# A gated mix of linear attention and a bilinear GLU: other h blocks in the joint products, no negated copies of o in DRAM, PSUM banks taken by age, the last two joint products behind the last unit

## The chip, the cores and the metric

The kernel runs on one core of one Trainium2 chip. The core has a matrix engine (TensorE, PE in the profile, with its weight loads as PEld), a vector engine (VectorE, DVE), a scalar engine (ScalarE, ACT), GpSimd (POOL) and a queue engine (SyncE, SP) that only issues DMA transfers. POOL issues the transfers that add to their destination. Each engine works through its own instructions in the order in which they stand, and waits for others through semaphores. The metric is the device time of one execution in microseconds, taken as the median of several runs.

## The reference

With x of 2048 x 512, everything in float32:

```
g = sigmoid((x * gate_w).sum(-1))                 # one number per row
q, k, v = x @ wqkv, split into 32 heads of 16     # phi(t) = where(t > 0, t + 1, exp(t)) + 1e-6
kv = phi(k)^T v per head;  z = sum of phi(k)
o = phi(q) kv / (phi(q) z + 1e-6)
a = o @ wo                                        # 512 x 512
h = (x @ w_gate) * (x @ w_up)                     # 512 -> 1792 columns
b = h @ w_down                                    # 1792 -> 512
out = g * a + (1 - g) * b
```

So a linear attention and a bilinear feed-forward layer read the same x, and their outputs are mixed by a gate.

## The kernel before

**Three products for one.** Every float32 operand is split into a high part (float32r) and the remainder, and a product is made of three matmuls: high x high, high x low, low x high (`mm3`, line 94). Splits cost one copy on ACT and one subtraction on VectorE.

**Seven products for eight.** Products of blocks of 2 x 2 are made by Strassen's scheme in Winograd's form: sums of blocks are formed first, seven products are taken, and their results are combined. This is done in two places.

**Units.** After a first phase (k, v and the attention's state), the work is a list `order` of 32 units, 16 for each half of the rows of x (pair 0 is units 0 to 15, pair 1 units 16 to 31). A unit (`unit`, line 415) makes one block of 128 columns: an `f` unit one block of h (both the gate and the up projection), a `q` unit two blocks of q. In pair 1 the units are f0, q0, f1, f2, f3, q1, f4 to f13, that is, the q units are 17 and 21, and f4 to f7 are units 22 to 25. The seven products go to four banks Y, X, R and S, in the order Y, X, Y, R, X, R, S, each of six matmuls of 512 columns. Between them ACT copies `m` (from the first Y) and `cross` (from the second Y and the second X), and VectorE forms `t`, the R and the S sums. Thus a delay of ACT at `m` stops the second Y, and a delay of `cross` stops the next use of the bank X or Y.

**Places.** Side work is hung on named places in a unit: `low`, `e`, `m`, `c`, `d`, `t`, `s`, `r`, `end`, in this order. `later(n, place, fn)` registers it, `do(n, place)` performs it. `d` is where the weights of the unit after next are prepared: `w_add` (line 165) has ACT scale and copy in the tile `wr`, which SP loaded at the end of the unit before (`w_load`, line 158), and then POOL adds other blocks into it by DMA.

**Down jobs.** Two f blocks of h and their rows of w_down make a group, and a group is 8 down jobs (`down_jobs`, line 649), one for each 128 rows of the output: six matmuls of 512 columns (two blocks, three each) into one bank `pdn`, which VectorE then adds to the sum `acc` in SBUF, scaled by 1 - g. Each unit performs as many as `shares` (line 407) gives for its four spots: after the first X (`many[0]`), after the second Y, after the second X, and before the second R.

**Attention.** A q unit leaves phi(q). In the next units the denominators are formed through DRAM (`terms`, `den`), and four tiles `rb` come back; VectorE multiplies them with phi(q) to give o (`norm_end`, line 744), and SP stores o in DRAM (`opark`). For the blocks 11 and 22 of o ACT also makes a negated copy in the tile `phq`, stored as `-11` and `-22`. For the last q unit of pair 1 these steps fall in units 24 and 25.

**Joint products.** The product of o with its weight (wo folded into the attention's state, blocks `wraw` in DRAM) is again a 2 x 2 scheme of seven products (`OPROD`, line 51; `products`, line 772). In pair 1 the scheme is shared with four h blocks, `MIXED` (line 37), f4 to f7, which go through the same combination: h is scaled by (1 - g)/g (`keep_scale`), so that one accumulation holds both. Those four units get no down jobs; their h stays in the tiles `hraw`. In pair 1 a joint product is four jobs of twelve matmuls of 256 columns, two with h (kind `h`) and two with o (kind `o`), into two banks `po`; then VectorE adds the banks to `acc`. Two of the seven continue in the banks of the one before. Each job k has its steps: the weight is loaded by SP (`w_raw`), added to by POOL (`w_sum`) and split (`w_split`); the o block is loaded by SP (`load`, k - 5), added to by POOL (`add`, k - 3) and split (`ready`, k), where k counts steps of five to a unit in pair 1 and four in pair 0. `step0` (line 775) says where step 0 lies: in pair 1 the place `e` of unit 26.

**Rings.** Tiles of one tag share a ring of buffers: `z`, `ph` (four each) and `cb` (three) hold `rb`, phi(q), the loaded o blocks `oraw` and the weights `wraw` in turn. A load into a ring waits until the buffer's last user is done, stores to DRAM included, and whatever stands behind it in SP's queue waits too.

**Banks.** Beside Y, X, R and S there are four PSUM banks, two with the tag `dn` and two with `att`. Down jobs and joint products take them by alternating the tag (`banks.reverse()`, line 668 and line 853), within the tag in turn.

**The end.** Behind the last unit stand the low parts of its h and the 8 down jobs of the last group (lines 994 to 998).

Of the kernel before, what the change touches and what calls it, by code (L numbers as in the profile page):

```python
# [14 lines left out]
P = 128  # L15
S = 2048
D = 512
# [19 lines left out]
MIXED = ((), (4, 5, 6, 7))  # L37
# [26 lines left out]
def gated_mix(ctx: ExitStack, tc, xt, xp, x, wqkv, wq, wq_add, wo, wgu, wgu_add, wdn, gate_w, out):  # L64
# [326 lines left out]
    ojobs, passed = [], [0]  # L391

# [251 lines left out]
    banks = ["dn", "dn"]  # L644
# [4 lines left out]
    def down_jobs(pair, group):  # L649
# [3 lines left out]
        def job(i):  # L653
# [12 lines left out]
            for o in range(0, D, step):  # L666
                cols = slice(o, o + step)
                banks.reverse()
                pd = psum.tile([P, D], F32, tag=banks[0], name="pdn", bufs=2)[:, 0:step]
                for j, (((_, hh), (_, hl)), (_, w2)) in enumerate(group):  # L670
                    mm3(pd, (hh[:, c, sl], hl[:, c, sl]), [w2[:, v, cols] for v in range(2)], j == 0, j == 1)
                a = acc[pair, i // 2][:, i % 2, cols]
                if first:
                    act(a, pd, scale=s)
                else:
                    stt(a, pd, s, a, ALU.mult, ALU.add)
                if ends:
                    to = nc.gpsimd if pair == 0 else nc.sync
                    tc.keep_in_program_order(to.dma_start(out[t * P:(t + 1) * P, cols], a))
            todo[0] -= 1  # L680
            if not todo[0]:
# [7 lines left out]
             for b in ("11", "12", "21", "22", "-11", "-22")}  # L689

    def attention(pair, j, n):
# [80 lines left out]
    def products(pair, n0):  # L772
        raw, tiles, wt, bank = {}, {}, {}, {}
        steps = STEPS[bool(MIXED[pair])]
        step0 = len(steps) * n0 + (0 if MIXED[pair] else 2)
# [13 lines left out]
        def load(k):  # L789
            p, kind, i = line[k]  # L790
            if kind == "o":
                dma(raw_tile(k).rearrange("p (r t) -> p r t", r=2), opark[pair, OPROD[p][2][0]][i])
# [36 lines left out]
        def ready(k, place):  # L829
            p, kind, i = line[k]  # L830
            tiles[k] = hi, lo = o_tiles()
            if k in raw:
                split(hi, lo, raw.pop(k))
            else:
                (block,) = OPROD[p][2]
                sign = -1.0 if block[0] == "-" else 1.0
                act(hi, row(block, i), scale=sign)
                if sign > 0:
                    tt(lo, row(block, i), hi.bitcast(F32), ALU.subtract)
                else:  # L840
                    stt(lo, row(block, i), -1.0, hi.bitcast(F32), ALU.mult, ALU.subtract)
            ojobs.append((passed[0] - (place == "end"), lambda: job(k)))

        def job(k):
# [5 lines left out]
            def product(h, s, lhs, r, starts, stop):  # L850

                if starts and not goes_on and s == 0:
                    banks.reverse()
                    bank[h] = psum.tile([P, 2, HALF], F32, tag=banks[0], name="po", bufs=2)
                mm3(bank[h][:, s], lhs, [v[:, r] for v in w2], starts and not goes_on and s == 0, stop, True)
# [11 lines left out]
            for block, sign in sums:  # L867
                m, c = int(block[0]) - 1, int(block[1]) - 1
                a = acc[pair, 2 * c + i][:, :, m * HALF:(m + 1) * HALF]
                tt(a, a, bank[i], ALU.add if sign > 0 else ALU.subtract)  # L870
# [91 lines left out]
    half = None  # L962
    for n, (pair, kind, m) in enumerate(order):
        entry = {}
        if n == 4:

            banks[0] = "att"
# [27 lines left out]
    down(0)  # L995
# [54 lines left out]
```

## Time and profile before

| | |
|---|---|
| median of 3 runs | 616.66 us (616.22 to 617.41) |
| profiled execution | 615.53 us, of which its span 613.8 us |
| TensorE busy | 598.3 us, 97% |
| VectorE busy | 461.9 us, 75% |
| ScalarE busy | 332.7 us, 54% |
| mean granted TensorE clock | 0.997 |
| moved by DMA | 116.04 MB, mean 189 GB/s |

The span runs from the first to the last instruction. A row of a timeline gives the start and the length in us, the engine, the line (L72 is the matmul's helper, L78 that of activations, L81 and L84 those of VectorE, L102 and L105 the two for transfers), the tiles as output<-inputs, and in brackets the idle time of that engine before the instruction, with what ended it. Tiles have the program's names without numbers. A row of the windows gives the stretch, its length, the busy time of PE, PEld, DVE, ACT and POOL with the instructions of each, the granted clock, the busy share of the DMA engines and GB/s. A row of waits gives the total, the count and the longest. Unit n starts with its first Y product, `bY<-xah`: unit 24 at 440.23, unit 25 at 451.11, unit 26 at 462.07, unit 27 at 487.03, unit 31 at 575.31.

### The profile page before, as it was taken

The page shows a single profiled execution, that of the slowest core. Times are in us where ns is not written, and L with a number is a line of the kernel's source. Part 1 is how long each engine was busy: PE and PEld are TensorE (multiplying, and loading weights), DVE is VectorE, ACT ScalarE, POOL GpSimd, SP SyncE. Part 2 cuts the span into 40 slices and gives each one's busy share as a digit, 9 for nine tenths or more (in the row PEclk, how much of TensorE's full clock was granted, in tenths as well). Part 3 has the DMA queues.
Part 4 walks back from the last instruction along what each step waited for, and adds up shares of the span by engine and source line. Part 5 has one row for each costly group of instructions (what it writes and reads, how often), then busy time and mean ns, then how long its engine had stood idle before and what let it go on. Part 6 is the DMA issues. An engine that isn't in the chain of part 4 may idle for free. (4 is left out here: it accounts for less than half of the span.)

```text
span 613.8 us, 8334 instructions
## 1 busy us (share of the span) xinstructions
PE 598.3 (97%) x2898; PEld 499.2 (81%) x2898; DVE 461.9 (75%) x736; ACT 332.7 (54%) x580; POOL 76.2 (12%) x95
## 2 busy tenths in 40 slices
PE   9999999999999999999999999999996989999997
PEld 6888888888888888888888888887874878888885
DVE  6877896756787788787789976677884777778955
ACT  3856756579546745453635567568353555345320
POOL 0011100000111110222201220001003311211000
PEclk9999999999999999999999999999998999999999
DMA  9467949657779878999688857687769988844003
GB/s 298 163 196 134 289 94 274 155 166 199 210 173 272 209 198 230 281 255 211 180 218 235 178 154 197 180 237 183 175 161 286 235 194 215 207 77 104 2 0 137
DMA packets 65803, 116.04 MB, mean 189 GB/s; under 512 B 7969, under 2 KB 29985, under 8 KB 65697
## 3 DMA queue, kind: packets, MB, share of 16 engines
q1 hardware_dynamic: 52816, 77.50, 38.1%
q0 software_dynamic: 12656, 37.49, 34.1%
q10 hardware_dynamic: 288, 0.52, 0.3%
q8 instruction: 22, 0.36, 0.2%
q14 instruction: 21, 0.16, 0.1%
HBM read 97.65 MB, written 19.94 MB: 192 GB/s over the span
## 5 line engine op out<-in xcount | busy, mean ns | idle before, releaser
L72 PE MATMUL pdn<-slot,slot 128*128 128x512 f32 (+1 forms) x582 | 144.9, 388 | 0.9 <-DVE slot L81 0.9
L72 PEld LDWEIGHTS pdn<-slot,slot 128*128 128x128 f32 x582 | 107.4, 188 | 23.2 <-DVE slot L81 1.6
L84 DVE SCALAR_TENSOR_TENSOR acc<-pdn,gate,acc 128x512 f32<-128x512 f32 (+1 forms) x81 | 59.7, 741 | 22.3 <-PE pdn L72 21.7
L81 DVE TENSOR_TENSOR wcl<-wr,wch 128x512 fp32r<-128x512 f32 (+1 forms) x96 | 73.4, 773 | 1.6 <-ACT wch L78 1.4
L78 ACT ACTIVATE slot<-cross 128x512 fp32r<-128x512 f32 x48 | 30.2, 629 | 81.1 <-DVE cross L81 81.1
L78 ACT ACTIVATE wch<-wr 128x512 fp32r<-128x512 f32 (+1 forms) x96 | 60.5, 695 | 0.7 <-DMA wr<-in_wgu_add 0.6
L72 PE MATMUL bX<-xbh,wch 128*128 128x512 f32 x128 | 50.3, 393 | 4.0 <-ACT cross L78 4.0
L105 POOL DMA_DIRECT2D wr<-in_wgu_add x28 | 24.1, 859 | 222.4 <-ACT wr L78 174.1
L72 PE MATMUL bX<-xbh,wcl 128*128 128x512 f32 x128 | 50.3, 393 | 0.0
L72 PE MATMUL bX<-xbl,wch 128*128 128x512 f32 x128 | 50.3, 393 | 0.0
L72 PE MATMUL po<-owh,oh 128*128 128x256 f32 x168 | 47.4, 282 | 1.7 <-DVE acc L81 1.7
L72 PE MATMUL po<-owh,ol 128*128 128x256 f32 x168 | 47.8, 285 | 0.8 <-DVE ol L81 0.8
L72 PE MATMUL po<-owl,oh 128*128 128x256 f32 x168 | 47.5, 283 | 0.0
L78 ACT ACTIVATE cross<-bY 128x512 f32<-128x512 f32 x32 | 19.1, 597 | 48.2 <-PE bY L72 48.0
L78 ACT ACTIVATE wr<-wr 128x512 f32<-128x512 f32 x64 | 36.6, 623 | 12.7 <-DMA wr<-in_wgu 9.4
L81 DVE TENSOR_TENSOR t<-bR,cross 128x512 f32<-128x512 f32 x32 | 22.1, 690 | 27.2 <-PE bR L72 18.2
L78 ACT ACTIVATE cross<-bX 128x512 f32<-128x512 f32 x32 | 19.0, 595 | 33.3 <-DVE bS L81 33.3
L81 DVE TENSOR_TENSOR bR<-bX,m 128x512 f32<-128x512 f32 x32 | 22.3, 697 | 19.0 <-PE bX L72 16.2
L72 PEld LDWEIGHTS po<-owh,oh 128*128 128x128 f32 x168 | 32.1, 191 | 3.3 <-DVE acc L81 1.9
L72 PEld LDWEIGHTS po<-owl,oh 128*128 128x128 f32 x168 | 32.1, 191 | 1.4
L81 DVE TENSOR_TENSOR slot<-cross,slot 128x512 fp32r<-128x512 f32 x48 | 32.8, 683 | 0.6
L72 PEld LDWEIGHTS po<-owh,ol 128*128 128x128 f32 x168 | 32.1, 191 | 1.3 <-DVE ol L81 1.2
(179 smaller groups left out, 1413.3 us busy)
## 6 DMA issues: line engine op xcount, KB each, us to landing
wr<-in_wgu_add POOLq DMA_DIRECT2D x28, 640.0 KB, 6.6
wr<-in_wgu SPq DMA_DIRECT2D x28, 384.0 KB
wdr<-in_wdn SPq DMA_DIRECT2D x24, 256.0 KB
oraw<-opark POOLq DMA_DIRECT2D x20, 256.0 KB, 7.1
xraw<-in_x SPq DMA_DIRECT2D x16, 256.0 KB
terms<-zq SPq DMA_DIRECT2D x16, 256.0 KB
zt<-terms SPq DMA_DIRECT2D x16, 256.0 KB
rb<-den SPq DMA_DIRECT2D x16, 256.0 KB
```

The lines of the kernel that those rows point to most:

```text
L72: tc.keep_in_program_order(nc.tensor.matmul(*args, **kw))
L78: pin(nc.scalar.activation(dst, src, func, **kw))
L81: pin(nc.vector.tensor_tensor(dst, a, b, op=op))
L84: pin(nc.vector.scalar_tensor_tensor(dst, a, scalar, b, op0=op0, op1=op1))
L105: tc.keep_in_program_order(nc.gpsimd.dma_start(dst, src, accum_op=ALU.add))
```

## The change

Five edits:

- `MIXED` names the h blocks 2, 3, 6 and 7 in place of 4 to 7. Blocks 4 and 5 (units 22 and 23) become an ordinary group with down jobs, 2 and 3 (units 19 and 20) have none. The table `shares` is written anew for pair 1: units 17 to 25 now have 2, 1, 1, 2, 1, 2, 2, 2, 3 down jobs (before: 3, 0, 4, 4, 1, 1, 1, 1, 0), units 26 and 27 two and one (before two each), units 28 to 31 four each as before.
- The joint products of pair 1 lie one step later (`step0`).
- The negated copies of o (`-11`, `-22`) are no longer made or stored. Where a joint product needs one and adds another block to it, the loaded block is negated in place by ACT before POOL's add; where it stands alone, its high part is copied with a factor of -1 and its low part formed accordingly.
- The four banks are four fixed tiles in a list. A down job takes the first and puts it at the end; a joint product takes two out and puts them back after its last sum.
- The last two joint jobs of pair 1 (the o jobs of the seventh product) are kept back until after the last unit, where they stand behind the low part of one half of the last h and ahead of the first closing down job. In unit 31, the order of the joint jobs and the down jobs is otherwise kept.

```diff
-MIXED = ((), (4, 5, 6, 7))
+MIXED = ((), (2, 3, 6, 7))
...
     ojobs, passed = [], [0]
+    LAST = 1 << 20
...
-    shares.update({units: (1, 2, 1, 2), units + 1: (1, 1, 1, 0)})
-    shares.update({units + m: (0, 1, 0, 0) for m in range(5, 9)})
-    shares.update({units + 9: (0, 0, 0, 0), units + 10: (0, 1, 0, 1), units + 11: (0, 1, 0, 1)})
+    shares.update({units + m: v for m, v in ((0, (1, 2, 1, 2)), (1, (0, 1, 1, 0)), (2, (0, 1, 0, 0)),
+                                             (3, (0, 1, 0, 0)), (4, (0, 1, 0, 1)), (5, (0, 1, 0, 0)),
+                                             (6, (0, 1, 0, 1)), (7, (1, 1, 0, 0)), (8, (0, 1, 0, 1)),
+                                             (9, (1, 1, 0, 1)), (10, (0, 1, 0, 1)), (11, (0, 1, 0, 0)))})
...
-    banks = ["dn", "dn"]
+    banks = []
+    def banks_there(tag):
+        banks.extend(psum.tile([P, D], F32, tag=tag, name=f"{tag}{i}", bufs=2) for i in range(2))
...
-                banks.reverse()
-                pd = psum.tile([P, D], F32, tag=banks[0], name="pdn", bufs=2)[:, 0:step]
+                there = banks.pop(0)
+                banks.append(there)
+                pd = there[:, 0:step]
...
-             for b in ("11", "12", "21", "22", "-11", "-22")}
+             for b in ("11", "12", "21", "22")}
...
             o_there(f"{j + 1}{c + 1}", r, den[i])
-            if j == c:
-                act(phs[r, c], den[i], scale=-1.0)
-                o_there(f"-{j + 1}{c + 1}", r, phs[r, c])
...
-        step0 = len(steps) * n0 + (0 if MIXED[pair] else 2)
+        step0 = len(steps) * n0 + (1 if MIXED[pair] else 2)
...
             if kind == "o":
+                if len(OPROD[p][2]) == 2 and OPROD[p][2][0][0] == "-":
+                    act(raw[k], raw[k], scale=-1.0)
                 for block in OPROD[p][2][1:]:
                     dma_add(raw[k].rearrange("p (r t) -> p r t", r=2), opark[pair, block][i])
...
+            src = raw.pop(k) if k in raw else row(OPROD[p][2][0], i)
+            if OPROD[p][2] == ("-22",):
+                act(hi, src, scale=-1.0)
+                stt(lo, src, -1.0, hi.bitcast(F32), ALU.mult, ALU.subtract)
             else:
...
+                split(hi, lo, src)
+
+            ends = MIXED[pair] and k >= last - 2
+            ojobs.append((LAST if ends else passed[0] - (place == "end"), lambda: job(k)))
...
                 if starts and not goes_on and s == 0:
-                    banks.reverse()
-                    bank[h] = psum.tile([P, 2, HALF], F32, tag=banks[0], name="po", bufs=2)
+                    there = banks.pop(0)
+                    bank[h] = there, there.rearrange("p (s c) -> p s c", s=2)
...
+            if p + 1 == len(OPROD) or not OPROD[p + 1][3]:
+                banks.append(bank[i][0])
...
     do(n, "low1")
-    down(0)
+    passed[0] += LAST
+    o_down()
     down(1)
     do(n, "low0")
     down(len(jobs))
```

More of the change, by code (lines that the diff above doesn't have):

```diff
@@ L852, in product @@
                 if starts and not goes_on and s == 0:
[L853 to L855 removed]
+                    there = banks.pop(0)
+                    bank[h] = there, there.rearrange("p (s c) -> p s c", s=2)
+                mm3(bank[h][1][:, s], lhs, [v[:, r] for v in w2], starts and not goes_on and s == 0, stop, True)
             if kind == "h":
@@ L965, in gated_mix @@
         if n == 4:
-            banks[0] = "att"
+            banks_there("att")
         def down_weights(n=n, entry=entry):
```

15 lines of the change are left out of this document (3 added, 12 removed).

## The prediction

> **What bounds the kernel now.** I read the page's head, then TensorE's own timeline for its idle gaps, then for the largest gap the rows of the engine named and of the queue behind it, and last the windows of DMA.
>
> ```profile
> span 613.8 us, 8334 instructions
> PE 598.3 (97%) x2898; PEld 499.2 (81%) x2898; DVE 461.9 (75%) x736; ACT 332.7 (54%) x580; POOL 76.2 (12%) x95
> ```
>
> TensorE is busy 97% of the span, so only what it stands still for can be won. These are all its stops that its timeline marks; the first is the start of the program, the bracket gives the idle time before the instruction and who ended it. The chain's rows behind them give the length of one product (six matmuls of 512 columns), of one joint-product job (twelve of 256), and of the closing down jobs.
>
> ```profile
> 336.93 0.39 PE L72 MATMUL po<-owh,ol 128*128 128x256 f32 x1 [0.18 <-DVE ol L81]
> 420.81 0.50 PE L72 MATMUL bY<-xc4h,wch 128*128 128x512 f32 x1 [0.49 <-ACT m L78]
> 455.14 0.50 PE L72 MATMUL bY<-xc4h,wch 128*128 128x512 f32 x1 [1.15 <-ACT m L78]
> 467.56 0.69 PE L72 MATMUL bX<-xbh,wch 128*128 128x512 f32 x1 [3.97 <-ACT cross L78]
> 469.75 0.63 PE L72 MATMUL bX<-xbh,wcl 128*128 128x512 f32 x1
> 472.14 0.51 PE L72 MATMUL bY<-xc4h,wch 128*128 128x512 f32 x1 [1.76 <-ACT m L78]
> 475.99 0.39 PE L72 MATMUL po<-owh,ol 128*128 128x256 f32 x1 [0.61 <-DVE ol L81]
> 493.87 0.39 PE L72 MATMUL po<-owh,oh 128*128 128x256 f32 x1 [1.65 <-DVE acc L81]
> 599.12 0.50 PE L72 MATMUL pdn<-slot,slot 128*128 128x512 f32 x1 [0.22 <-DVE slot L81]
> 600.32 10.15 PE L72 MATMUL pdn<-slot,slot 128*128 128x512 f32 x49 [0.70 <-DVE slot L81]
> ...
> 497.57 1.43 PE po L72 x12
> 500.39 1.36 PE bX L72 x6
> ```
>
> The stops add up to 10.73 us, and 10.06 of them lie behind 455 us, in units 25 to 27 and at the end. One cost is not in the brackets: the six matmuls from 467.56 to 469.75 start 0.438 us apart, where a product normally takes 1.36 us, 0.227 each. That is 6 x 0.211 = 1.27 us more, behind the one gap of 3.97 us.
>
> By the Trainium skill (TensorE: Matmul & The Clock Gate, section on the HAM clock gate) TensorE falls to half its clock once a window of some 3.4 us passes idle, and needs about as long at work to come back. The trace agrees as to which gap does it: 3.97 us did, 1.76 and 1.65 did not. By the page's figures such a slow stretch would lose an estimated 1.7 us and the sum below would win 0.4 us more; the rows say 1.27, and that is used.
>
> Now the cause of the 3.97 us. ACT's rows, then the start of unit 24 on TensorE and the second block of o on VectorE with SP's rows, then POOL's, a wait of SP and the size of a transfer:
>
> ```profile
> 447.75 1.15 ACT L78 ACTIVATE wr<-wr 128x512 f32<-128x512 f32 x2 [0.87 <-DMA wr<-in_wgu]
> 453.97 0.63 ACT L78 ACTIVATE phq<-rb 128x512 f32<-128x512 f32 x1 [0.57 <-DVE rb L84]
> 454.51 0.58 ACT L78 ACTIVATE m<-bY 128x512 f32<-128x512 f32 x1
> 465.87 1.15 ACT L78 ACTIVATE wr<-wr 128x512 f32<-128x512 f32 x2 [6.16 <-DMA wr<-in_wgu]
> 466.93 0.58 ACT L78 ACTIVATE cross<-bX 128x512 f32<-128x512 f32 x1
> 470.98 0.63 ACT L78 ACTIVATE owh<-wraw 128x512 fp32r<-128x512 f32 x1 [3.47 <-DMA wraw<-in_wdn]
> ```
> ```profile
> 440.23 0.39 PE L72 MATMUL bY<-xah,wch 128*128 128x512 f32 x1
> 452.06 0.68 DVE L84 SCALAR_TENSOR_TENSOR rb<-phq,rb 128x512 f32<-128x512 f32 x1
> ...
> 444.64 0.40 SPq L102 DMA_DIRECT2D wr<-in_wgu  x1
> 450.69 0.38 SPq L102 DMA_DIRECT2D opark<-rb  x1
> 458.71 0.38 SPq L102 DMA_DIRECT2D wraw<-in_wdn  x1
> 460.22 0.48 SPq L102 DMA_DIRECT2D wr<-in_wgu  x1
> ```
> ```profile
> 463.12 1.20 POOL L105 DMA_DIRECT2D wraw<-in_wdn  x1 [13.07 <-DMA wraw<-in_wdn]
> 559.52 1.73 POOL L105 DMA_DIRECT2D oraw<-opark  x2 [13.20 <-DMA oraw<-opark1-22_989]
> ```
> ```profile
> SPq L102 <- DMA opark<-rb: 8.0, 2, 7.6
> ```
> ```profile
> opark1-22_989<-phq SPq DMA_DIRECT2D x2, 256.0 KB
> ```
>
> SP issues the store of the first block of o at 450.69 and then nothing until 458.71: the next transfer, the first h weight of the joint products, takes a buffer of the ring `z` that this store still reads, and waits 7.6 us for it to land. Unit 27's weights `wr` stand behind it, leave at 460.22, and ACT waits 6.16 us for them with `cross` behind in its queue; TensorE needs `cross` and stops 3.97. The stops of 1.76 and 0.61 follow from the same lateness: the weight's add leaves POOL at 463.12 and lands at 470.98. The 1.15 at 455.14 is another thing: ACT's `m` comes behind two negated copies of o, `phq<-rb`, which wait for VectorE's `rb`.
>
> **The change part by part.** The counts of TensorE, VectorE and ACT instructions stay as they are; only places change, so TensorE's work is the same and the sum is over its stops.
>
> *No negated copies.* Eight activations and eight stores of 256 KB go, half of them in pair 1. With the two at 453 to 454.5 gone, `m` comes when its product ends: 1.15 us goes. In exchange eight activations on loaded o blocks appear, in units 14, 15, 30 and 31, two steps (two fifths to half of a unit) after the place of their load, at 0.6 us each, with `cross` or `m` queued behind them on ACT and TensorE waiting for those. ACT is busy 54% of the span: nothing if the load has landed, the first rival if not.
>
> *Joint products one step later, blocks 2, 3, 6, 7.* Unit 24's SP order becomes: store of the first o, store of the second, `wr`, store of the third, and only then the weight that waits for the first store. The load of `wr` is no longer behind the wait. How much time has it? Units are 7 x 1.36 us and 1.37 per down job; unit 24 has two in the new order (12.3 us), unit 25 three (13.6). In the old trace the first `rb` store leaves at 450.69, 10.5 us after unit 24's start at 440.23; the second o is made by 452.74, 12.5, and comes 0.75 later for one more eviction ahead of it; with the issues `wr` leaves at about 13.8, which is 1.6 us into unit 25. ACT asks for it when Y, X, a down job, Y, `cross` and three copies of weights are through, 8.0 into unit 25: 6.4 us. The load that left at 444.64 was there at 447.75, 3.1 us; as slow as the store's 7.6 it would be 1.2 late, and ACT has 6.16 - 3.97 = 2.2 us of slack. So 3.97 and its 1.27 of slow clock go.
>
> What is late next is the first joint weight. Its buffer comes free at 10.5 + 7.6 = 18.1 from unit 24's start, 5.8 into unit 25; its load took 458.71 to 463.12, 4.4, and its add 463.12 to 470.98, 7.9: there at 18.1 into unit 25, which is 4.5 into unit 26. ACT asks for it at 2.5 and stands some 2 us. TensorE first needs it behind Y X Y D R X, at 8.2, and with copy, `cross`, copy and low part at 0.5 to 0.7 each it is ready at about 7.0: no stop. But ACT's delay goes on through three copies of `wr`, two sums, and two more copies (4.4 us) to the second joint job, ready at about 11.4 to 12.2 where TensorE arrives at 11.0. I put 1.2 us there, in the place of 1.76 + 0.61. Bounds: nothing, if the add lands a quarter sooner than under the old trace's load; 5.5 us, from the second rival.
>
> *1.65 at 493.87.* There a joint job follows directly on the one whose sum VectorE must read from the same bank. In the new order Y, a down job and half a joint job (1.36 + 1.37 + 0.7 us) lie between, against 0.7 for the sum: it goes.
>
> *Banks by age.* A tile is now fixed to a bank and taken when it was longest free. Its users wait for the same readers. Where two banks are held by joint products, down jobs alternate on the other two, and each return to a bank has at least 4 us in between (three jobs) against 0.75 for its eviction: nothing. With fewer jobs between it would cost what is missing to some 1.5 us each.
>
> *Down jobs of units 16 to 27.* The same 56 of pair 0 end one unit later; units 19 and 20 lose five jobs, 22 to 25 win six. The weight loads of units 18 to 21 then meet units of 10.9 us, as those of units 21 to 24 did before, where only 0.49 was lost. I keep 0.49 and 0.18: nothing won, nothing lost (bound: 0.5 once more).
>
> *Last two joint jobs behind the last unit.* They give TensorE 2 x 1.43 = 2.86 us while VectorE and ACT finish the last h:
>
> ```profile
> 597.72 0.61 ACT L78 ACTIVATE slot<-wdr 128x512 fp32r<-128x512 f32 x1
> 599.58 0.68 DVE L81 TENSOR_TENSOR slot<-cross,slot 128x512 fp32r<-128x512 f32 x1
> 605.00 0.75 DVE L84 SCALAR_TENSOR_TENSOR acc<-pdn,gate,acc 128x512 f32<-128x512 f32 x1 [0.61 <-PE pdn L72]
> ```
>
> The low part that the first closing job awaits is done at 600.26, 2.5 us behind the last product's end at some 597.7, so 0.22 + 0.70 = 0.92 goes. Four sums of 0.6 each join VectorE's tail; it idles 0.61 of every 1.36 us there, and eight jobs give back 4.9: the end behind the last matmul stays.
>
> *Sum.* 1.15 + 3.97 + 1.27 + 1.76 + 0.61 + 1.65 + 0.92 = 11.33 goes, 1.2 comes: 10.1 us. The profiled execution took 615.53 us for its span of 613.8, and lies 1.1 below the median of 616.66; so 605.4 against its own time, and 606.5 as a median.
>
> **The rivals.**
>
> *Slower: the negations on ACT wait for their loads.* ACT's queue is in order, as 465.87 and 466.93 show: `cross` ran only when the wait of 6.16 was over. Before, POOL took these waits. If each of the eight negations stands w us, TensorE loses about w - 2.2 each time. From w = 3.5 us on the gain is gone (8 x 1.3 = 10.4), and at 5 it is 616.7 - 10.1 + 22.4 = 629. For it speaks POOL's row at 559.52, 13.2 us for just such a block. Against it: that counts from POOL's last work, not from when the block was due.
>
> ```profile
> 298.12 0.46 SPq L102 DMA_DIRECT2D oraw<-opark0-11_982  x1
> 302.44 1.13 ACT L78 ACTIVATE wr<-wr 128x512 f32<-128x512 f32 x2
> 555.39 1.26 SPq L102 DMA_DIRECT2D oraw<-opark1-22_989  x2
> 576.92 0.58 ACT L78 ACTIVATE m<-bY 128x512 f32<-128x512 f32 x1
> 579.66 0.63 ACT L78 ACTIVATE owh<-wraw 128x512 fp32r<-128x512 f32 x1 [1.64 <-PE po L72]
> ```
>
> The pair-1 loads of 555.39 land by 559.52 and are due near 575 to 577; the tightest is 298.12, due behind 302.44 + 1.1, 5.4 us against 4.1 for 555.39's. So 0.10 and no more. The Trainium skill (TensorE: Matmul & The Clock Gate, architectural detail) calls ScalarE's and VectorE's queues strictly first in, first out; the rows above agree.
>
> *DMA is the limit.* Part of the stops may only be the shape in which a full DMA shows.
>
> ```profile
> 435.00:455.00 20.00, 18.99 (x83) 15.13 (x81) 17.90 (x29) 8.81 (x16) 1.71 (x2) 1.00 0.61 156
> 455.00:490.00 35.00, 28.52 (x135) 23.25 (x136) 22.47 (x35) 14.14 (x27) 10.59 (x11) 0.95 0.98 242
> ```
>
> From 455 to 490 its engines were busy 98% and moved 242 x 35 = 8.47 MB. Without 0.5 MB of negated copies 7.97 MB are left, 32.9 us at that rate, and the new order gives them 35 - 7.6 = 27.4: 5.5 us would stay in the place of my 1.2, 610.8. Against it: in the 20 us before, DMA was at 61%, because SP stood; the new order issues stores and loads there. 0.22.
>
> *Nothing changes.* The wait for the store may only move and some other load that ACT awaits stand behind it; then units 25 to 27 keep their 10 us and the end wins 0.9: 615.7 to 616.7. The order speaks against it, since `wr` stands ahead. 0.05.
>
> **How the numbers follow.** Forecast (606.5, alone 604.8 to 608.5): 0.58. DMA-bound, 608.5 to 612.5: 0.22. A small win above 612.5, of new stops that I don't see: 0.05. Within 0.2%, 1.2 us, which is about what this measurement tells from no change: 0.05. Slower: 0.10. The range 604.0 to 612.5 holds the first two; its lower end is all stops of units 25 to 27 and the end gone (605.3), and 0.67 and the runs' own scatter on top. Faster 0.85.
>
> **What the changed profile would show.** Right: no stop of TensorE over 1.5 us behind 455 us, clock 1.00 throughout, SP's `wr` of unit 27 issued within 2 us of unit 25's start, no `phq<-rb` on ACT, the closing down jobs without a stop. Wrong: a stop in unit 26 with ACT on `owh<-wraw` for over 3 us (DMA-bound); an ACT row `oraw<-oraw` with a wait for `opark` of more than 2 us (first rival); a stop `po` or `pdn` waiting for `acc` on VectorE (banks).

## The result and the profile after

The changed kernel took 607.46 us (median; 606.07 to 608.46), the kernel before 616.44 us beside it: a ratio of 0.985, with a 95% interval of 0.9825 to 0.9882. The forecast was 606.5 us in a range of 604.0 to 612.5. The profiled execution took 606.07 us, where the sum had given 605.4 for such an execution.

The head of the page of the changed kernel:

```profile
span 604.4 us, 8314 instructions
PE 595.6 (99%) x2898; PEld 497.8 (82%) x2898; DVE 461.9 (76%) x736; ACT 331.9 (55%) x580; POOL 76.3 (13%) x95
```

TensorE's timeline of the changed kernel, all stops that it marks behind the start of the program but two (0.34 us at 222.96 and 0.15 us at 386.20, both at a VectorE sum into the bank S):

```profile
336.50 0.39 PE L72 MATMUL att<-owh,ol 128*128 128x256 f32 x1 [0.18 <-DVE ol L81]
415.72 0.50 PE L72 MATMUL bY<-xc4h,wch 128*128 128x512 f32 x1 [2.02 <-ACT m L78]
472.84 0.39 PE L72 MATMUL att<-owh,ol 128*128 128x256 f32 x1 [0.22 <-DVE ol L81]
476.50 0.39 PE L72 MATMUL att<-owh,oh 128*128 128x256 f32 x1 [0.81 <-ACT oh L78]
477.31 0.39 PE L72 MATMUL att<-owh,ol 128*128 128x256 f32 x1 [0.30 <-DVE ol L81]
```

Of the ten microseconds behind 455, 1.33 are left, in unit 26, and nothing stands at the end; unit 22 has 2.02 where it had 0.49. The same two stretches of the windows as before:

```profile
435.00:455.00 20.00, 20.00 (x88) 15.92 (x87) 18.29 (x31) 8.42 (x15) 1.71 (x2) 1.00 0.68 172
455.00:490.00 35.00, 33.66 (x170) 28.12 (x169) 27.16 (x43) 17.17 (x31) 10.79 (x11) 1.00 1.03 243
```

The clock stays at 1.00. DMA is as full as it was (1.03 and 243 GB/s; before 0.98 and 242), and yet TensorE hardly stands. All five signs that the prediction named for being right are there, and none of those for being wrong: ACT's wait for `owh<-wraw` in unit 26, with 2.69 us, stays just under the 3 us that would have spoken for the DMA rival.

Where the 9.4 us of span went, by the starts of units, first the kernel before, then the changed one:

```profile
93.02 0.39 PE L72 MATMUL bY<-xah,wch 128*128 128x512 f32 x1
508.59 0.39 PE L72 MATMUL bY<-xah,wch 128*128 128x512 f32 x1
```
```profile
92.33 0.39 PE L72 MATMUL bY<-xah,wch 128*128 128x512 f32 x1
499.48 0.39 PE L72 MATMUL bY<-xah,wch 128*128 128x512 f32 x1
```

Unit 0 starts 0.69 sooner, ahead of anything that was changed; no edit of the change is at work there, and a_fewer, whose program is the same up to that point, starts it at 92.92. Unit 28 starts 9.11 sooner, but has one joint job (1.43) more still to come. So units 0 to 27 won 9.11 - 0.69 - 1.43 = 7.0, and the rest, 9.4 - 9.1 + 1.4 = 1.7, is won at the end. The marked stops agree with the first: 9.81 + 1.27 of slow clock before, 4.02 after, 7.06 less.

The queue behind the store of the first o, on SP, then ACT's rows, in the changed kernel:

```profile
448.68 3.11 SPq L102 DMA_DIRECT2D opark<-rb  x2
451.91 0.78 SPq L102 DMA_DIRECT2D wr<-in_wgu  x1
452.79 0.78 SPq L102 DMA_DIRECT2D opark<-rb  x1
455.85 0.37 SPq L102 DMA_DIRECT2D wraw<-in_wdn  x1
```
```profile
458.40 1.13 ACT L78 ACTIVATE wr<-wr 128x512 f32<-128x512 f32 x2
469.44 0.63 ACT L78 ACTIVATE owh<-wraw 128x512 fp32r<-128x512 f32 x1 [2.69 <-DMA wraw<-in_wdn]
```

`wr` leaves 1.5 us into unit 25 (which starts at 450.42) and ACT no longer waits for it. The first joint weight still waits for the store, until 455.85, and comes 2.69 us after ACT asks.

### The profile page after: what moved, and what is told of

It reads as the page before. It is cut to its first block, busy times and chain, and to the rows that moved or that the text cites. A ratio compares the mean times of both kernels' runs of the same rounds, so it can differ in the third digit from the quotient of the medians.

```text
span 604.4 us, 8314 instructions
## 1 busy us (share of the span) xinstructions
PE 595.6 (99%) x2898; PEld 497.8 (82%) x2898; DVE 461.9 (76%) x736; ACT 331.9 (55%) x580; POOL 76.3 (13%) x95
## 4 chain that ended last, share of the span: by engine, by line
PE 83%; DMA 7%; DVE 5%; issue 2%; ACT 2%; SPq 0%; DVEq 0%; POOL 0%; ACTq 0%; POOLq 0%
PE dn L72 14%; PE att L72 13%; PE bY L72 12%; PE bR L72 11%; PE bX L72 11%; PE pk L72 7%; PE gt L72 7%; PE bS L72 6%; DMA wr<-in_wgu 2%; DMA wraw<-in_wdn 1%; DMA zt<-terms 1%; DMA wdr<-in_wdn 1%; DMA den<-den 1%; PE warm L72 1%; DMA rb<-den 1%
## 5 line engine op out<-in xcount | busy, mean ns | idle before, releaser
L72 PE MATMUL dn<-slot,slot 128*128 128x512 f32 (+1 forms) x336 | 83.0, 386 | 0.0
L72 PEld LDWEIGHTS dn<-slot,slot 128*128 128x128 f32 x336 | 61.7, 188 | 12.1
L72 PE MATMUL att<-slot,slot 128*128 128x512 f32 x246 | 62.3, 390 | 0.0
L72 PEld LDWEIGHTS att<-slot,slot 128*128 128x128 f32 x246 | 45.8, 188 | 9.3
L84 DVE SCALAR_TENSOR_TENSOR acc<-dn,gate,acc 128x512 f32<-128x512 f32 (+1 forms) x45 | 33.1, 737 | 9.1 <-PE dn L72 8.8
L84 DVE SCALAR_TENSOR_TENSOR acc<-att,gate,acc 128x512 f32<-128x512 f32 x36 | 26.9, 749 | 11.8 <-PE att L72 11.6
L78 ACT ACTIVATE m<-bY 128x512 f32<-128x512 f32 x32 | 19.1, 595 | 24.5 <-PE bY L72 24.4
L105 POOL DMA_DIRECT2D oraw<-opark x20 | 19.7, 1037 | 91.2 <-ACT oraw L78 27.8
L72 PE MATMUL att<-owh,ol 128*128 128x256 f32 x100 | 28.6, 286 | 0.7 <-DVE ol L81 0.7
```

What stands on the lines that cost most here:

```text
L72: tc.keep_in_program_order(nc.tensor.matmul(*args, **kw))
L78: pin(nc.scalar.activation(dst, src, func, **kw))
L84: pin(nc.vector.scalar_tensor_tensor(dst, a, scalar, b, op0=op0, op1=op1))
L105: tc.keep_in_program_order(nc.gpsimd.dma_start(dst, src, accum_op=ALU.add))
```

## The experiments

Kernels with b_ start from the kernel before, those with a_ from the changed one. Every ratio is to the kernel before, measured beside it. In the diffs, `...` stands for lines left out. One table shows what the explanation turns on: when SP issued the store of the first o, when ACT was free for the first joint weight (its row's start less its idle time), when it got it, and what TensorE's timeline then marks in units 26 and 27. Times are us.

| kernel | store of first o | ACT asks | ACT gets it | store to weight | stops there |
|---|---|---|---|---|---|
| before | 450.69 | 467.51 | 470.98 | 20.3 | 3.97 1.76 0.61 1.65 |
| b_ncph | 451.43 | 463.35 | 468.39 | 17.0 | 0.47 4.50 |
| b_thin | 452.07 | 460.75 | 465.37 | 13.3 | 1.72 0.58 0.27 |
| b_step0 | 453.24 | 467.39 | 476.18 | 22.9 | 5.87 |
| a_step0 | 448.36 | 463.98 | 469.32 | 21.0 | 4.41 |
| a_mixed | 450.63 | 463.35 | 474.03 | 23.4 | 7.43 |
| a_fewer | 450.31 | 464.28 | 474.30 | 24.0 | 7.11 |
| changed | 448.68 | 466.75 | 469.44 | 20.8 | 0.22 0.81 0.30 |
| a_ph | 449.77 | 467.61 | 469.87 | 20.1 | 0.81 0.31 |
| a_notail | 447.97 | 466.20 | 471.21 | 23.2 | 2.10 0.22 |
| a_q21ph | 447.84 | 465.00 | 468.85 | 21.0 | 0.94 0.23 0.82 0.31 |
| a_best | 449.36 | 467.41 | 472.12 | 22.8 | 0.45 0.22 0.72 0.31 |
| a_early | 449.69 | 467.74 | 467.74 | 18.1 | 0.64 0.31 |

One caution for reading it: a_notail is the changed kernel up to the last unit, and yet its weight comes 23.2 us behind the store and not 20.8, and its stops in unit 26 are 2.32 us and not 1.33. So differences of 1 us in a stop, or of 2.4 us in the weight's time, between two single profiles can come without any edit.

**b_nocopies: the kernel before without the negated copies.**

```diff
-            if j == c:
-                act(phs[r, c], den[i], scale=-1.0)
-                o_there(f"-{j + 1}{c + 1}", r, phs[r, c])
...
+                if len(OPROD[p][2]) == 2 and OPROD[p][2][0][0] == "-":
+                    act(raw[k], raw[k], scale=-1.0)
...
```

> The kernel before with one edit: the negated copies of o are neither made nor stored, ACT negates the loaded blocks as in the change. Theory (stops of TensorE that hang on single waits): the 1.15 us at 455.14 goes, perhaps some tenths more from the shorter SP queue, and everything behind the store of the first o stays (a stop of 3 to 4 us at X, the slow clock, the follow-ups, the 1.65): 1 to 2 us faster than before, 614.4 to 615.4. Rival (DMA is the limit between 455 and 490): 0.5 MB less in that stretch at 242 GB/s is 2.2 us less, and as much of the 0.5 MB of pair 0 as is not hidden: 2 to 4.3 us faster, 612 to 614.4. Rival (negations on ACT wait for their loads): no faster, or slower by up to 10 us.

615.3 us, 0.9975 (0.9955 to 0.9994). The 1.15 at `m` of unit 25 is gone, the other stops stay (the 3.97 is 4.58 in this profile), and no negation on ACT waits. That is 1.5 us by the ratio, with 0.4 to 2.8 as its interval: the theory's 1 to 2 lies in it, and so does the lower end of the DMA rival's 2 to 4.3. What is gone from TensorE's timeline is the 1.15 and nothing else, which speaks for the theory. The profiled execution itself is no shorter than that of before (its span is 614.9 us), because the 4.58 is longer and the clock is slow behind the 1.66 at 493.37 too (see the last section); so the win rests on the medians. The rival of waiting negations is out.

**b_ncph: in addition, no wait for the store.**

```diff
-            tag = ("z", "ph")[p % 2] if kind == "h" else "cb"
+            tag = ("z", "ph")[p % 2 if p else 1] if kind == "h" else "cb"
```

> The kernel before without negated copies (as b_nocopies), and the first weight of the joint products takes a buffer of the ring ph in the place of the ring z. With no negated copies these buffers are free as soon as VectorE has made o, so this load has no store to wait for; queue order, jobs and bytes are those of b_nocopies. Theory (the wait of SP for the store is the cause of the 3.97, of the slow clock, and of the follow-ups): SP issues this weight at 449 to 452 and unit 27's wr at once behind it and the second store; 3.97 + 1.27 go, and most of 1.76 + 0.61: 5.5 to 8 us faster than b_nocopies, 607 to 609.5. Rival (DMA is the limit): the same bytes, so the stops stay in another shape: 0 to 2 us faster than b_nocopies. Rival (the wait only moves): a stop of 2 us or more on another load in units 25 to 27, 2 to 4 us faster than b_nocopies.

612.68 us, 0.9928 (0.99 to 0.9956): 2.6 us less than b_nocopies and not 5.5 to 8. SP's issues, POOL's add and ACT's row of this kernel, and its two stops of unit 26:

```profile
451.43 0.38 SPq L102 DMA_DIRECT2D opark<-rb  x1
451.85 1.03 SPq L102 DMA_DIRECT2D wraw<-in_wdn  x1
```
```profile
460.57 1.20 POOL L105 DMA_DIRECT2D wraw<-in_wdn  x1 [9.82 <-DVE wcl L81]
```
```profile
468.39 0.63 ACT L78 ACTIVATE owh<-wraw 128x512 fp32r<-128x512 f32 x1 [5.04 <-DMA wraw<-in_wdn]
```
```profile
463.40 0.50 PE L72 MATMUL bX<-xbh,wch 128*128 128x512 f32 x1 [0.47 <-ACT cross L78]
469.56 0.50 PE L72 MATMUL bY<-xc4h,wch 128*128 128x512 f32 x1 [4.50 <-ACT m L78]
```

SP waits for nothing, the 3.97 is 0.47, as the theory has it. But the weight, whose load leaves 0.4 us behind the store and not 8.0, is added to only at 460.57 and there at 468.39: 17.0 us behind the store, 3.3 sooner than before. TensorE now reaches unit 26 on time and stands 4.50 there. The third alternative, that the wait moves, is the one that the rows show and whose 2 to 4 us came; by the intervals alone the 0 to 2 us of the DMA rival are not excluded. A stop of 1.18 us in unit 23, which the kernel before does not have, stays unexplained.

**b_thin: b_ncph with less traffic.**

```diff
+            if n in (26, 27):
+                dma_add(raws[n][:, 2:3, 0:16], src[:, 0:1, 0:16])
...
+                    c = 16 if MIXED[pair] and k < 5 else HALF
...
+                c = 16 if MIXED[pair] and j == 1 else HALF
...
```

> The kernel of b_ncph, in which the waiting of SP for the store is gone and yet a stop of 4.50 us stood at m in unit 26, with the first joint weight there only at 468.39, 7.8 us behind the issue of its add at 460.57. Left out here (the result is not the reference's for it): nearly all columns of five other adds of POOL that travel at that time, those into the h weights of units 26 and 27 (640 KB each), into the second joint weight and into the first two o blocks (256 KB each): some 2 MB less between 450 and 475. Theory (the time of the transfers is set by what else the DMA engines carry): load and add of the first weight land 2 to 4 us sooner, the stop at m is 0.5 to 2.5 in the place of 4.50, and the time is 2 to 5 us below that of b_ncph, 608 to 610.5. Rival (an add takes some 8 us from issue to landing whatever else goes on): the first weight's add lands 7 to 8 us behind its issue as before, the stop stays at 4 to 4.5, within 1 us of b_ncph, 611.7 to 613.5.

608.42 us, 0.9861 (0.984 to 0.9882), 4.3 us below b_ncph. The load and the add of the first weight together took 12.9 us (452.50 to 465.37) in the place of 16.5:

```profile
457.89 1.20 POOL L105 DMA_DIRECT2D wraw<-in_wdn  x1 [7.06 <-DVE rb L84]
```
```profile
466.54 0.50 PE L72 MATMUL bY<-xc4h,wch 128*128 128x512 f32 x1 [1.72 <-ACT m L78]
```

Most of the gain lies between the load's issue and the add's (5.4 us, 8.7 in b_ncph); the add itself took 7.5 against 7.8, as the rival said. When the load landed no row shows: in both kernels POOL's row names a VectorE instruction as what ended its wait, while the program gives this add only the load to wait for. With 4.3 us less in the time, the run shows that what the DMA engines carry besides does set when the weight comes; whether through the load or through the time at which POOL issues the add stays open. That part of the DMA rival is right.

**b_step0: the kernel before, one step later.**

```diff
-        step0 = len(steps) * n0 + (0 if MIXED[pair] else 2)
+        step0 = len(steps) * n0 + (1 if MIXED[pair] else 2)
```

> The kernel before with one edit: the joint products of pair 1 lie one step later. The blocks stay 4 to 7, so unit 25 has one down job and not three. Theory: wr is ahead of the wait and the 3.97 with the slow clock goes, as does the 1.65; but the first joint weight is still there only some 12.3 us (load 4.4, add 7.9) behind the landing of the store at 458.3, that is at 471, where ACT asks for it at 464 to 465 and TensorE's first joint job stands at 469 to 470: a stop of 3 to 4.5 us with its follow-ups stays. Altogether 3 to 6 us faster than before, 610.5 to 613.5: the step alone does only half, the down jobs moved in by the other blocks do the rest. Rival (the step does it all, the blocks nothing): 8 to 9 us faster, 607.5 to 608.5. Rival (DMA is the limit): 0 to 2 us faster, 614.5 to 616.5.

613.63 us, 0.9941 (0.992 to 0.9962), 3.6 us by the ratio. `wr` leaves ahead of the wait (456.43), the 3.97 and the 1.65 are gone, and 5.87 stands at the joint job, more than the 3 to 4.5 expected: the weight was there at 476.18, 5 us later than reckoned. Of these, 2.9 come from the load, which left only at 461.20 (reckoned 458.3), and the rest from load and add, which took 15.0 us and not 12.3.

**a_step0: the changed kernel at the old step** (the same line, back to 0).

> The changed kernel with one edit: the joint products of pair 1 begin at the old step, unit 26's place e. The blocks 2, 3, 6, 7 and their down jobs stay. Theory: the first joint weight is there at the same 469.4, but is asked for a step (some 2.2 us) sooner, with m behind it on ACT: a stop of about 4 us at m of unit 26, perhaps the slow clock behind it, up to 1 us for wr that stands behind the wait again, and 1.65 back at the joint job that follows the one whose sum it needs: 4 to 7 us slower than the changed kernel, 611.5 to 614.5. Rival (DMA is the limit, or the blocks alone do it): the place of a step makes no odds, within 1 us of the changed kernel, 606.5 to 608.5.

609.53 us, 0.9875 (0.9846 to 0.9904): 1.3 us above the changed kernel by the ratios, between the two forecasts; the two intervals overlap, so this difference is not clear of the noise.

```profile
470.49 0.79 PE L72 MATMUL bY<-xc4h,wch 128*128 128x512 f32 x1 [4.41 <-ACT m L78]
```

The stop at `m` came as expected (4.41 for some 4), with the slow clock; but `wr` cost nothing, the 1.65 did not return, unit 22 had 1.21 and not 2.02, and behind the 4.41 nothing stands where the 1.33 was.

**a_mixed: the changed kernel with the old blocks and the old table of down jobs.**

```diff
-MIXED = ((), (2, 3, 6, 7))
+MIXED = ((), (4, 5, 6, 7))
...
```

> The changed kernel with the old blocks 4 to 7 and the old table of down jobs; the later step, no negated copies, banks by age and the held back joint jobs stay. Unit 25 has one down job again in the place of three, unit 24 one in the place of two. Theory (the weight is there some 20 us behind the store of the first o in every order, and what counts is how late TensorE asks for it): with 4 us fewer of down jobs in between a stop of 3 to 5 us stands in unit 26 where 1.33 stood, and the 2.02 of unit 22 is 0.49: 1 to 3 us slower than the changed kernel, 608.5 to 610.5, 6 to 8 us below before. Rival (the blocks and their down jobs do nothing, the step and the missing copies do it all): within 1 us of the changed kernel, 606.5 to 608.5. Rival (the blocks are all of it): 614 to 615.5.

613.22 us, 0.9935 (0.9914 to 0.9956), 5 us above the changed kernel, more than expected: the stop is 7.43.

**a_fewer: the new blocks, but one down job in units 24 and 25.**

```diff
-                                             (6, (0, 1, 0, 1)), (7, (1, 1, 0, 0)), (8, (0, 1, 0, 1)),
-                                             (9, (1, 1, 0, 1)), (10, (0, 1, 0, 1)), (11, (0, 1, 0, 0)))})
+                                             (6, (0, 1, 0, 1)), (7, (1, 1, 0, 0)), (8, (0, 1, 0, 0)),
+                                             (9, (0, 1, 0, 0)), (10, (0, 1, 0, 1)), (11, (1, 1, 1, 1)))})
```

> The changed kernel; units 24 and 25 have one down job each (two and three in the changed kernel), and the three go to unit 27. The blocks 2, 3, 6, 7, the later step and the order of all transfers stay. Theory (the first weight is there some 20 us behind the store of the first o, and the down jobs between that store and the joint products are what covers it): ACT asks for the weight about 4.1 us sooner while it comes when it came, TensorE stands 4 to 7 us at the first joint job of unit 26 in the place of 1.33, and with the slow clock the kernel is 3 to 6 us slower than the changed one, 610.5 to 613.5; that is nearly the whole of what a_mixed lost. Rival (it is the blocks themselves, other rows of h ready sooner, that matter): within 1 us of the changed kernel, 606.5 to 608.5.

613.69 us, 0.9934 (0.9914 to 0.9955): the same 5 us as a_mixed, with the blocks, the step and the order of all transfers of the changed kernel. TensorE's row, ACT's, and a window of TensorE, whose clock is the third number from the end:

```profile
476.96 0.58 PE L72 MATMUL dn<-owh,oh 128*128 128x256 f32 x1 [7.11 <-ACT oh L78]
```
```profile
474.30 0.63 ACT L78 ACTIVATE owh<-wraw 128x512 fp32r<-128x512 f32 x1 [10.02 <-DMA wraw<-in_wdn]
```
```profile
465.00:480.00 15.00, 7.89 (x35) 6.51 (x34) 6.35 (x11) 4.83 (x9) 2.94 (x4) 0.81 1.02 242
```

This says what the new blocks are worth: as far as the intervals tell (some 1.3 us either way), their whole effect is that three more down jobs may stand between the first o and the joint products. From the store to ACT's asking 14.0 us pass here, 18.1 in the changed kernel: 4.1 us, three jobs of 1.37. The weight itself came 3.2 us later behind the store than in the changed kernel; a_notail, with all its down jobs in place, has 2.4 us of that too, so it is not shown to be an effect of this edit.

**a_notail: the last joint jobs not held back.**

```diff
-            ends = MIXED[pair] and k >= last - 2
+            ends = False
```

> The changed kernel, with the last two joint jobs of pair 1 in unit 31 again and not behind the last unit. Theory: the stops of 0.23 and 0.70 ahead of the closing down jobs are back and nothing else is, 0.9 to 1.6 us slower than the changed kernel, 608.4 to 609. Rival (VectorE's tail of four more sums costs what the stops cost): no difference.

608.29 us, 0.985 (0.9829 to 0.9871): no difference. The end of this kernel and, behind it, of the changed one:

```profile
590.22 0.28 PE L72 MATMUL dn<-owh,oh 128*128 128x256 f32 x1
...
591.65 1.76 PE L72 MATMUL dn<-slot,slot 128*128 128x512 f32 x6
593.25 2.91 PE L72 MATMUL att<-slot,slot 128*128 128x512 f32 x12
```
```profile
589.86 1.55 PE L72 MATMUL dn<-slot,slot 128*128 128x512 f32 x6
591.24 2.88 PE L72 MATMUL att<-slot,slot 128*128 128x512 f32 x12
```

One joint job stands behind the last S anyway, since all of them lie a step later. The first closing job then takes 1.60 us from start to start against 1.38. So with the later step in place, holding back both jobs is worth 0.2 us. Holding back is of use by itself, though: a_step0 has the jobs held back at the old step, and there the first closing job takes 1.39 us (594.86 to 596.25) and nothing is lost at the end either. Each of the two edits hides most of the end's loss without the other.

**a_ph: no wait for the store in the changed kernel** (the edit of b_ncph).

> The changed kernel; the first joint weight takes a buffer of the ring ph in the place of z, so that its load (455.85 in the changed kernel) has no store to wait for and follows wr at 452.5 to 453.5. Theory: the weight is there 1.5 to 3 us sooner than 469.44 (in b_ncph the same step brought 3 us), ACT waits for it 0 to 1.2 us in the place of 2.69, and the 1.33 us of unit 26 shrinks to 0.3 or less: 0.7 to 1.3 us faster than the changed kernel, 606.2 to 606.8. Rival (the DMA engines are full from 452 on, so the weight lands when it lands): 1.0 to 1.4 us stay in unit 26, no difference.

605.55 us, 0.9821 (0.9796 to 0.9845). In unit 26 0.81 and 0.31 stay: the rival is right there, though POOL's rows show another reason than its. The load left 1.2 us sooner (454.66), but POOL issued the add at 461.21, behind unit 27's add at 460.67, as in the changed kernel (460.42 behind 459.82). The time is below the forecast, but its interval and that of the changed kernel overlap, and no stop in unit 26 explains it; a stop of 1.32 us in unit 21 is even new.

**a_q21ph and a_best: down jobs moved for unit 22, and in a_best for unit 26.**

```diff
-                                             (3, (0, 1, 0, 0)), (4, (0, 1, 0, 1)), (5, (0, 1, 0, 0)),
-                                             (6, (0, 1, 0, 1)), (7, (1, 1, 0, 0)), (8, (0, 1, 0, 1)),
+                                             (3, (0, 1, 0, 0)), (4, (0, 1, 0, 1)), (5, (0, 1, 0, 1)),
+                                             (6, (0, 1, 0, 0)), (7, (1, 1, 0, 0)), (8, (0, 1, 0, 1)),
...
```

In a_best besides:

```diff
-                                             (9, (1, 1, 0, 1)), (10, (0, 1, 0, 1)), (11, (0, 1, 0, 0)))})
+                                             (9, (1, 1, 0, 1)), (10, (0, 2, 0, 1)), (11, (0, 0, 0, 0)))})
```

> The kernel of a_ph with one down job of unit 22 moved to the end of unit 21. In the changed kernel m of unit 22 came 2.02 us late, because ACT got unit 23's wr only at 409.5 and then worked without a gap through twelve activations to m at 415.04. Theory: the job gives ACT 1.37 us, the stop of 2.02 is 0.5 to 0.8 and no other takes its place; with the ring ph 2 to 2.7 us faster than the changed kernel, 604.8 to 605.5. Rival (unit 22, one job shorter, now waits at its own m or in unit 23): a stop of 1 us or more between 420 and 440, no faster than a_ph.

> The changed kernel with two down jobs moved: one of unit 22 to the end of unit 21, and the one of unit 27 into unit 26, behind its second Y and ahead of the first joint job. Theory: the 2.02 of unit 22 is 0.7 as in a_q21ph; the weight's lateness then shows in unit 26 (2.30 in a_q21ph), but the job moved in covers 1.37 of it, so about 0.9 stays: 1.5 to 2.5 us faster than the changed kernel, 605 to 606. Rival (each gain is given back at the next late weight): a stop of 1 to 2 us in unit 27 or 28, which has a job less, and no difference to the changed kernel.

606.15 us, 0.9831 (0.9806 to 0.9857), and 607.86 us, 0.9846 (0.9825 to 0.9866): both miss their forecast, and neither is shown to be faster than what it started from. Unit 22 has 0.70 in a_q21ph and 1.53 in a_best, with the same edit there; in a_early, below, 2.09. Without the edit it was 2.02 (changed), 1.31 (a_ph), 1.25 (a_notail), 1.21 (a_step0) and 1.89 (a_fewer). The moved job brings an activation of 0.67 us into ACT's unbroken row, and the stop seems to follow when the transfers for unit 23 land. a_best still has 1.70 us in unit 26, where 0.9 was expected, and 0.83 in unit 23, where the changed kernel has none. In a_q21ph, what was won in unit 22 came back in unit 26 (2.30), whose weight did not come sooner.

**a_early: load and add of the first weight one step earlier, on a_q21ph.**

```diff
-                    at_step(k, lambda place, j=j: fn(j))
+                    at_step(k - (bool(MIXED[pair]) and j == 0 and ahead > 0), lambda place, j=j: fn(j))
```

> The kernel of a_q21ph (the ring ph for the first joint weight, one down job from unit 22 to the end of unit 21), with the load and the add of this weight one step earlier; it is split at the same place. So SP issues the load right behind the store of the first o, with nothing to wait for, and POOL issues the add ahead of unit 27's add of 640 KB in the place of behind it. Theory (in the changed kernel and in a_ph the weight is late because its add stands in POOL's queue behind that of wr, issued at 460, and shares the DMA engines with it): add at 456 to 458 as in b_thin and b_ncph, some 8 us to land, there at 464 to 466 where ACT asks at 465 to 466.7: the stops of unit 26 (2.30 in a_q21ph) shrink to 1.1 or less, 1 to 1.5 us faster than a_q21ph; unit 27's wr may come 1 us later without a stop. Rival (DMA full, the weight lands when it lands): at 468 to 470 as in every run, 2 us or more stay in unit 26, within 0.5 us of a_q21ph.

604.79 us, 0.9814 (0.9793 to 0.9835). The add left POOL at 459.10, later than the 456 to 458 expected, for the load took 9.0 us (450.12 to 459.10), but ahead of unit 27's at 461.67, and for once ACT did not wait for the weight:

```profile
467.74 0.62 ACT L78 ACTIVATE owh<-wraw 128x512 fp32r<-128x512 f32 x1
```
```profile
476.88 0.39 PE L72 MATMUL att<-owh,oh 128*128 128x256 f32 x1 [0.64 <-ACT oh L78]
477.69 0.38 PE L72 MATMUL att<-owh,ol 128*128 128x256 f32 x1 [0.31 <-DVE ol L81]
```

Unit 26's 2.30 is 0.95, as expected; what is left hangs on VectorE's sums of h: ACT waited 1.83 us for one at 471.82, and went from there without a gap to the `oh` that TensorE awaited. This kernel has the lowest time of all, but its interval and that of the changed kernel overlap, so it is not shown to be faster.

## Why the prediction was right, point by point

One slip of reading changes no sum: the first row of the prediction's list of stops is not the start of the program, which the list does not hold.

- **No negated copies, 1.15.** Right: b_nocopies won 1.5 us (0.4 to 2.8). Eight activations `oraw<-oraw` appeared on ACT and none has a wait, so the slower rival did not happen.
- **3.97 and 1.27, `wr` behind the store's wait.** Both went, and the times given for `wr` held (1.6 us into unit 25 expected, 1.5 measured). But the wait was not the whole cause. Without it, in the old order, 4.50 us and a slow stretch stand one place further on (b_ncph). What made the win is the row of the working that was used only to see how late the weight would be: two and three down jobs in units 24 and 25. Without these three the kernel loses 5 of its 9 us (a_fewer, a_mixed); the step alone, without them, gives 3.6 (b_step0), and on top of them 1.3, which is not clear of the noise (a_step0).
- **1.2 in unit 26.** Measured 1.33. The weight was expected 4.5 us into unit 26 and came at 5.4 (464.02 to 469.44), ACT stood 2.69 for some 2.
- **1.65.** It went, but adjacency alone was not the reason. b_ncph has the order of before, and there unit 27 takes 5.91 us from its first Y to its second, against 1.36 + 1.36 + 2 x 1.43 = 5.58: 0.33 lost; b_thin has 0.27, and a_step0 no such stop. The rest was VectorE, behind in its queue: in the kernel before its rows go without a gap from 484.60 on to the sum that TensorE awaited at 493.87. That it was behind because of the late weight is likely, not shown.

```profile
493.13 0.68 DVE L81 TENSOR_TENSOR acc<-acc,po 128x512 f32<-128x512 f32 x1
```

- **0.49 kept in unit 22.** Mis-sized: 2.02. ACT got unit 23's `wr` at 409.51, some 8 us behind its issue at 401.41, and went without a gap through copies and eight activations of the q unit to `m` at 415.04. The working said that units 18 to 21 would be as units 21 to 24 had been; it left out that unit 21 is a q unit, and that the first down jobs of a sum are emptied by ACT. It makes the forecast 1.5 us too low; the next point (0.7 the other way) and the 0.69 of unit 0 make up most of that. So it is partly luck that the profiled execution came within 0.7 us of the sum.
- **0.92 at the end.** Mis-sized: from start to start the end had lost more than its brackets say. The first closing job was cut in pieces of 4, 1 and the rest, at 597.55, 599.12 and 600.32; at 0.227 us a matmul that is 0.66 + 0.97 = 1.63. And the gain is not the holding back's alone, as the working had it: the later step by itself leaves 0.2 of it (a_notail), the holding back by itself nothing (a_step0).
- **Banks by age.** No row of the changed kernel waits for a bank at a joint or down job. The edit was not tried by itself.
- **The DMA rival, 610.8.** It did not come, for DMA is as full as before with 1.33 us of stops. But its mechanism is real: with some 2 MB less the weight came 3.7 us sooner behind its issue, and the kernel was 4.3 us faster than b_ncph (b_thin). Traffic makes the weight late; the down jobs give it the time. The two theories were not alternatives.

## What to carry to other kernels

When one late transfer stops the chain, ask not only what holds its issue, but when its result would come without that, and what the consumer would then wait for: removing a wait of 7.6 us won 2.6. With DMA full, what worked here was independent work between the first moment at which the transfer can start and its use. Keeping its parts ahead of other transfers in each queue ended ACT's wait in one profile (a_early), but is not shown to save time. Stops near a late transfer can be its echoes, and brackets on a timeline can understate a stop; starts of equal work tell it better. And one edit should not be judged by a single profile's stop of 1 us.

## What the runs showed of the hardware

An add of 256 KB by POOL landed much later where the DMA engines were full. From the list of DMA issues of the changed kernel, first from 570 to 604 us, where 77 GB/s were moved, then from 450 to 490, 242 GB/s (the last number is us from issue to landing, of one add and the median of three):

```profile
oraw<-opark POOLq DMA_DIRECT2D x1, 256.0 KB, 4.0
```
```profile
wraw<-in_wdn POOLq DMA_DIRECT2D x3, 256.0 KB, 9.0
```

For the bytes they move, adds take more of the engines. The changed kernel from 440 to 480 us, by queue (packets, MB, share of the engines; the first is POOL's, the second SP's):

```profile
q0 software_dynamic: 1358, 3.03, 46.8%
q1 hardware_dynamic: 4168, 6.23, 45.0%
```

That is 15.4% a MB against 7.2%, so by this measure an add cost here like a plain transfer of twice its size.

The clock was the other surprise. Stops of 3.97 us and more were each followed by a slow stretch, but the shorter ones cannot be told by their length. The kernel before ran on at full clock behind the 1.65 us at 493.87; b_nocopies has the same stop with 1.66 us and did not. The second Y behind it and the job that follows, first in the kernel before, then in b_nocopies, with the stop:

```profile
494.67 0.40 PE L72 MATMUL bY<-xc4h,wch 128*128 128x512 f32 x1
496.05 1.29 PE L72 MATMUL pdn<-slot,slot 128*128 128x512 f32 x5
```
```profile
493.37 0.49 PE L72 MATMUL po<-owh,oh 128*128 128x256 f32 x1 [1.66 <-DVE acc L81]
494.72 0.63 PE L72 MATMUL bY<-xc4h,wch 128*128 128x512 f32 x1
497.12 1.54 PE L72 MATMUL pdn<-slot,slot 128*128 128x512 f32 x6
```

The same six matmuls took 1.38 us in the one and 2.40 in the other. In unit 22 the changed kernel's 2.02 us cost no clock, while 1.89 in a_fewer and 2.09 in a_early did. The changed kernel's window behind its stop, then the rows of a_early and a window (the clock is the third number from the end):

```profile
417.00:420.00 3.00, 3.00 (x15) 2.49 (x14) 0.10 (x1) 3.00 (x6) 0.00 (x0) 1.00 0.72 237
```
```profile
416.63 0.50 PE L72 MATMUL bY<-xc4h,wch 128*128 128x512 f32 x1 [2.09 <-ACT m L78]
418.99 2.23 PE L72 MATMUL att<-slot,slot 128*128 128x512 f32 x6
421.07 0.40 PE L72 MATMUL bR<-xc1h,wch 128*128 128x512 f32 x1
```
```profile
418.00:420.00 2.00, 2.00 (x6) 1.51 (x6) 0.01 (x1) 2.00 (x4) 0.00 (x0) 0.50 0.46 81
```

In a_early the eleven matmuls from 416.97 to 421.07 took 4.1 us and not 11 x 0.227 = 2.5, so this stop cost 1.6 us beside its own 2.09; a_notail has such a stretch behind a stop of 2.10 in unit 26. The prediction read the one trace as if some length between 1.76 and 3.97 decided; it does not. What does decide, these runs do not show. The Trainium skill (TensorE: Matmul & The Clock Gate, section on the HAM clock gate) calls its window of some 3.4 us free-running, which would fit that like stops end differently; its rule that a whole window must be idle does not fit stops of 1.66 to 2.10 us.
